# Rewriting a two-block attention kernel: B's keys and values first, and one unit-by-unit schedule for sliding-window attention with the other products between

## The chip, the cores and the metric

One core of one Trainium2 chip runs the kernel. The metric is the device time of one execution in microseconds. The kernel before has a median of 465.69 us over 6 runs (463.81 to 466.82).

## The reference

Two independent blocks read their own x (2048 tokens, 640 channels, bf16) and write the two halves of an output of 2048 x 1280. Both project x to q, k and v with 32 heads of 20 channels.

Block A is attention in a window of 256 tokens; block B is linear attention:

```python
# A
scores = einsum("bhqd,bhkd->bhqk", q, k) * (Dh ** -0.5)
mask = (q_idx - k_idx >= 0) & (q_idx - k_idx < 256)
p = softmax(where(mask, scores, -1e9)); o = p @ v;  a = o @ wo
# B
phi = lambda t: where(t > 0, t + 1, exp(t)) + 1e-6
kv = einsum("bhsd,bhse->bhde", phi(k), v);  z = phi(k).sum(over tokens)
o = (phi(q) @ kv) / (phi(q) @ z + 1e-6);  b = o @ wo
```

## The kernel before, in words

The tile framework places instructions by a scheduler; the program text sets priority, and stages follow each other nearly as written.

1. `load_inputs` (L92) transposes x of A by DMA on the SP queue (L98) and loads wqkv and wo. It is called again for B before the attention.
2. `proj_channel_major` (L109) makes q and k of A with channels on partitions: 5 chunks of 4 x 5 matmuls of 512 columns (L129), an eviction of 2048 columns (L139, L141), and then small DMAs on three queues (L163) that move each head's 20 channels to a 32-partition slot of `q_pad` or `k_pad`. Four heads share a tile of 128 partitions.
3. `proj_token_major` (L165) makes v of A with tokens on partitions (L180, L190) and puts a column of ones behind each head's 20 channels, so that the product with v also gives the denominator.
4. The attention of A (L278 to L335) goes by 16 blocks of 128 queries and in each by steps of 3 heads: up to 9 score products of 128 columns with 20 rows (L288), one exponential of up to 1152 columns on ACT (L297), a mask product on DVE for the oldest key block (L301) and one for the diagonal block (L307), and 9 value products with the probabilities as weights and 21 columns (L317). Division by the denominator is at L325 and L328.
5. `tail` (L208) transposes A's output on TensorE (L220), evicts it (L224), multiplies with wo (L229), evicts (L237) and stores. B's queries (L129 again, with exp and relu at L144 and L146) run in the same stretch.
6. B's keys and values (L369), their phi (L378 to L390), the kv sum per group of four heads (L403, L412), the products with phi(q) (L426), the division (L435 to L439) and B's `tail`.

All of a stage's buffers are opened and closed with the stage. Scores have 2 PSUM buffers.

Of the kernel before, what the change touches and what calls it, by code (L numbers as in the profile page):

```python
# [8 lines left out]
P = 128  # L9
ALU = mybir.AluOpType  # L10
ACT = mybir.ActivationFunctionType
BF16 = mybir.dt.bfloat16
F32 = mybir.dt.float32


@with_exitstack
def kernel(
# [10 lines left out]
    nc = tc.nc  # L28
    _, S, D = A_x.shape
    H = 32  # L30
    Dh = D // H
    HD = 32
    HV = Dh + 1
    HG = H // 4
    KT = D // P
    NT = S // P
    NQ = 512
    NQT = S // NQ
    assert S % NQ == 0 and D % P == 0 and H * Dh == D and Dh < HD
    scale = float(Dh) ** -0.5  # L40
    out2 = out[0]
    xA = A_x[0]
    xB = B_x[0]

    def head_pieces(c):
        pieces = []
        for h in range(H):
            r0 = h * Dh
            r1 = r0 + Dh
            lo = max(r0, c * P)  # L50
            hi = min(r1, (c + 1) * P)
            if lo < hi:
                pieces.append((h, lo - c * P, hi - lo, lo - r0))
        return pieces

    head_steps = []
    h0 = 0
    while h0 < H:
        nh = min(3, H - h0)
        head_steps.append((h0, nh))  # L60
        h0 += nh

    const = ctx.enter_context(tc.tile_pool(name="const", bufs=1, side="left"))
    ident = const.tile([P, P], BF16, name="ident")
    make_identity(nc, ident[:])
    maskD = const.tile([P, P], BF16, name="maskD")
    nc.gpsimd.memset(maskD[:], 1.0)
    nc.gpsimd.affine_select(
        out=maskD[:],
        in_=maskD[:],  # L70
        pattern=[[1, P]],
        compare_op=ALU.is_ge,
        fill=0.0,
        base=0,
        channel_multiplier=-1,
    )
    maskE = const.tile([P, P], BF16, name="maskE")
    nc.gpsimd.memset(maskE[:], 1.0)
    nc.gpsimd.affine_select(
        out=maskE[:],  # L80
        in_=maskE[:],
        pattern=[[-1, P]],
        compare_op=ALU.is_ge,
        fill=0.0,
        base=-1,
        channel_multiplier=1,
    )
    woA_sb = const.tile([P, KT, D], BF16, name="woA_sb")
    woB_sb = const.tile([P, KT, D], BF16, name="woB_sb")
    otokA = const.tile([P, NT, D], BF16, name="otokA")  # L90

    def load_inputs(stack: ExitStack, name, x_ap, wqkv_ap, wo_ap, wo_tile):  # L92
        inp = stack.enter_context(tc.tile_pool(name=name, bufs=1, side="right"))
        xT = inp.tile([P, KT, S], BF16, name=f"xT_{name}")
        w = inp.tile([P, KT, 3 * D], BF16, name=f"w_{name}")
        xv = x_ap.rearrange("s (c p) -> s c p", p=P)
        for c in range(KT):
            nc.sync.dma_start_transpose(out=xT[:, c, :], in_=xv[:, c, :])  # L98
        wv = wqkv_ap.rearrange("(kt p) n -> p kt n", p=P)
        for i in range(3):  # L100
            nc.sync.dma_start(
                out=w[:, :, i * D : (i + 1) * D], in_=wv[:, :, i * D : (i + 1) * D]
            )
        nc.sync.dma_start(out=wo_tile[:], in_=wo_ap.rearrange("(kt p) n -> p kt n", p=P))
        return xT, w

    dma_engines = [nc.sync, nc.scalar, nc.gpsimd]

    def proj_channel_major(  # L109
        name, xT, w, col_base, pads, mode, psum_bufs, stage_bufs, sbuf_side="right"  # L110
    ):
        with ExitStack() as stack:
            psq = stack.enter_context(
                tc.tile_pool(name=f"psq_{name}", bufs=psum_bufs, space=bass.MemoryType.PSUM, side="left")
            )
            stage = stack.enter_context(
                tc.tile_pool(name=f"stage_{name}", bufs=stage_bufs, side=sbuf_side)
            )
            scr = None
            if mode == "phi":  # L120
                scr = stack.enter_context(
                    tc.tile_pool(name=f"scr_{name}", bufs=1, side=sbuf_side)
                )
            dcount = 0
            for c in range(KT):
                ps = psq.tile([P, NQT, NQ], F32, name="ps")
                for nt in range(NQT):
                    for kt in range(KT):
                        nc.tensor.matmul(  # L129
                            ps[:, nt, :],  # L130
                            lhsT=w[:, kt, col_base + c * P : col_base + (c + 1) * P],
                            rhs=xT[:, kt, nt * NQ : (nt + 1) * NQ],
                            start=(kt == 0),
                            stop=(kt == KT - 1),
                        )
                chunk = stage.tile([P, S], BF16, name="chunk")
                cv = chunk[:].rearrange("p (n f) -> p n f", f=NQ)
                if mode == "scale":
                    nc.scalar.activation(out=cv, in_=ps[:], func=ACT.Copy, scale=scale)  # L139
                elif mode == "copy":  # L140
                    nc.any.tensor_copy(out=cv, in_=ps[:])  # L141
                elif mode == "phi":
                    e = scr.tile([P, NQT, NQ], BF16, name="e")
                    nc.scalar.activation(out=e[:], in_=ps[:], func=ACT.Exp)  # L144
                    r = scr.tile([P, NQT, NQ], BF16, name="r")
                    nc.scalar.activation(out=r[:], in_=ps[:], func=ACT.Relu)  # L146
                    nc.vector.tensor_scalar(
                        out=cv,
                        in0=e[:],
                        scalar1=1e-6,  # L150
                        scalar2=1.0 + 1e-6,
                        op0=ALU.add,
                        op1=ALU.min,
                    )
                    nc.vector.tensor_tensor(out=cv, in0=cv, in1=r[:], op=ALU.add)
                else:
                    raise ValueError(mode)
                for h, src_row, cnt, dst_off in head_pieces(c):
                    hg, j = divmod(h, 4)
                    dst = pads[hg][HD * j + dst_off : HD * j + dst_off + cnt, :]  # L160
                    eng = dma_engines[dcount % len(dma_engines)]
                    dcount += 1
                    eng.dma_start(out=dst, in_=chunk[src_row : src_row + cnt, :])  # L163

    def proj_token_major(name, xT, w, col_base, dstv_fn, mode, psum_bufs):  # L165
        with ExitStack() as stack:
            pst = stack.enter_context(
                tc.tile_pool(name=f"pst_{name}", bufs=psum_bufs, space=bass.MemoryType.PSUM, side="left")
            )
            scr = None  # L170
            if mode == "phi":
# [94 lines left out]
    with ExitStack() as at:  # L266
# [8 lines left out]
        def oslot(h):  # L275
            return (h % 2) * 16 + h // 2
# [199 lines left out]
```

## Time and profile before

| | |
|---|---|
| median of 6 runs | 465.69 us (463.81 to 466.82) |
| profiled execution | 466.82 us, span 465.0 us |
| mean granted TensorE clock | 0.769 of full speed |
| TensorE (PE) busy | 391.0 us, 84% |
| weight loads (PEld) | 224.5 us, 48% |
| VectorE (DVE) | 195.2 us, 42% |
| ScalarE (ACT) | 274.7 us, 59% |
| GpSimd (POOL) | 25.8 us, 6% |
| DMA | 25.56 MB in 34,361 packets |

PE busy time covers overlapping matmuls with modelled ends, so it says that the engine was occupied and not that it ran at its peak. Busy shares are means over stages that differ a good deal, and have to be read stage by stage.

### The profile page before, as it was taken

How to read it: one execution, taken by the hardware profiler on the slowest of the kernel's cores; microseconds unless marked ns; L12 is line 12 of the kernel's file. 1: busy time of each engine (PE TensorE's matmuls, PEld its weight loads, DVE VectorE, ACT ScalarE, POOL GpSimd, SP SyncE). 2: the span in 40 equal slices, each digit the busy share in tenths (PEclk: the TensorE clock that was granted, in tenths of full speed). 3: DMA queues.
4: the chain of work that ended last, by engine and by line, in shares of the span. 5: the costliest groups of instructions: out<-in, count | busy, mean ns of one | idle time of the engine just before them, and what ended most of it. 6: DMA issues, size and time to landing. Idle time of an engine off the chain costs nothing. (4 is left out here: it accounts for less than half of the span.)

```text
span 465.0 us, 10106 instructions
## 1 busy us (share of the span) xinstructions
PE 391.0 (84%) x4316; PEld 224.5 (48%) x4316; DVE 195.2 (42%) x497; ACT 274.7 (59%) x322; POOL 25.8 (6%) x48
## 2 busy tenths in 40 slices
PE   0298989989999999999999999889866999839975
PEld 0143435545555556555555555444422555626542
DVE  0000151056665655566566666714411322228721
ACT  1034103589888898998888886651434767442222
POOL 1012221000000000000000002200101000000000
PEclk9999999965555555555555555999978999968999
DMA  8954351097000000000000000033221000001111
GB/s 162 301 167 130 81 138 54 1 207 234 1 3 1 4 2 1 3 1 1 4 2 1 3 1 1 30 92 114 88 79 53 4 0 1 1 1 43 58 62 67
DMA packets 34361, 25.56 MB, mean 55 GB/s; under 512 B 23180, under 2 KB 32396, under 8 KB 34316
## 3 DMA queue, kind: packets, MB, share of 16 engines
q1 hardware_dynamic: 31628, 19.65, 15.4%
q0 software_dynamic: 1632, 2.61, 2.3%
q10 hardware_dynamic: 1056, 2.66, 2.2%
q8 instruction: 34, 0.56, 0.5%
q14 instruction: 11, 0.09, 0.1%
HBM read 6.55 MB, written 5.24 MB: 25 GB/s over the span
## 5 line engine op out<-in xcount | busy, mean ns | idle before, releaser
L297 ACT ACTIVATE p<-S_ps 128x1152 bf16<-128x1152 f32 (+3 forms) x176 | 173.5, 1042 | 20.3 <-PE S_ps L288 16.2
L288 PE MATMUL S_ps<-q_pad,k_pad 20*128 20x128 bf16 x1440 | 116.9, 289 | 15.6 <-ACT p L297 13.7
L317 PE MATMUL O_qb<-vaugA,p 128*128 128x21 bf16 x1440 | 96.2, 185 | 1.6 <-DVE p L307 0.8
L317 PEld LDWEIGHTS <-p 128*128 128x128 bf16 x1440 | 64.4, 106 | 56.0 <-DVE p L301 27.0
L301 DVE TENSOR_TENSOR p<-p,maskE 128x384 bf16<-128x384 bf16 (+1 forms) x154 | 54.0, 351 | 57.6 <-ACT p L297 56.6
L307 DVE TENSOR_TENSOR p<-p,maskD 128x384 bf16<-128x384 bf16 (+1 forms) x176 | 60.8, 346 | 24.7 <-ACT p L297 24.2
L129 PE MATMUL ps<-xT_inA,w_inA 128*128 128x512 bf16 x200 | 46.0, 394 | 21.8 <-DMA w_inA<-in_A_wqkv_dram 19.8
L288 PEld LDWEIGHTS <-k_pad 20*128 20x128 bf16 x1440 | 46.1, 104 | 29.4 <-issue 18.9
L369 PE MATMUL pstkv<-w_inB,xT_inB 128*128 128x512 bf16 (+1 forms) x240 | 45.1, 352 | 3.8 <-ACT r L146 3.8
L237 ACT CAST osb<-pso 128x640 bf16<-128x640 f32 x25 | 17.4, 694 | 51.3 <-PE pso L229 39.1
L129 PEld LDWEIGHTS <-w_inA 128*128 128x128 bf16 x200 | 20.1, 101 | 47.2 <-DMA w_inA<-in_A_wqkv_dram 19.8
L229 PEld LDWEIGHTS <-oT_cmp 128*128 128x128 bf16 x320 | 24.1, 98 | 34.9 <-DVE oT_cmp L224 12.0
L369 PEld LDWEIGHTS <-xT_inB 128*128 128x128 bf16 x240 | 24.0, 100 | 25.1 <-issue 5.2
L141 DVE CAST chunk<-ps 128x2048 bf16<-128x2048 f32 x4 | 9.2, 2292 | 57.7 <-PE ps L129 57.7
L129 PE MATMUL ps<-xT_inB,w_inB 128*128 128x512 bf16 x100 | 28.9, 435 | 3.7 <-ACT r L146 3.7
L229 PE MATMUL pso<-woB_sb,oT_cmp 128*128 128x512 bf16 (+1 forms) x160 | 26.0, 305 | 6.1 <-DVE oT_cmp L224 4.8
L139 ACT ACTIVATE chunk<-ps 128x2048 bf16<-128x2048 f32 x5 | 9.4, 1877 | 34.5 <-PE ps L129 29.4
L229 PE MATMUL pso<-woA_sb,oT_cmp 128*128 128x512 bf16 (+1 forms) x160 | 24.5, 300 | 5.3 <-ACT oT_cmp L224 2.9
L190 ACT CAST vaugA<-pst 128x640 bf16<-128x640 f32 x14 | 9.7, 696 | 28.9 <-PE pst L180 28.9
L180 PE MATMUL pst<-w_inA,xT_inA 128*128 128x512 bf16 (+1 forms) x160 | 21.9, 299 | 2.4 <-DVE chunk L141 2.4
L378 ACT ACTIVATE et<-pstkv 128x640 bf16<-128x640 f32 x16 | 11.3, 704 | 14.8 <-PE pstkv L369 14.8
L224 DVE COPY oT_cmp<-T 128x640 bf16<-128x640 bf16 x22 | 10.8, 489 | 20.5 <-PE T L220 20.3
(47 smaller groups left out, 240.6 us busy)
## 6 DMA issues: line engine op xcount, KB each, us to landing
out_dram<-osb SPq DMA_DIRECT2D x32, 160.0 KB
w_inA<-in_A_wqkv_dram SPq DMA_DIRECT2D x3, 800.0 KB
w_inB<-in_B_wqkv_dram SPq DMA_DIRECT2D x3, 800.0 KB
woA_sb<-in_A_wo_dram SPq DMA_DIRECT2D x1, 800.0 KB
woB_sb<-in_B_wo_dram SPq DMA_DIRECT2D x1, 800.0 KB
q_pad<-chunk SPq DMA_DIRECT2D x10, 80.0 KB
q_pad<-chunk POOLq DMA_DIRECT2D x10, 80.0 KB, 3.8
k_pad<-chunk SPq DMA_DIRECT2D x10, 80.0 KB
```

The source lines that it names most:

```text
L129: nc.tensor.matmul(ps[:, nt, :], lhsT=w[:, kt, col_base + c * P : col_base + (c + 1) * P], rhs=xT[:, kt, nt * NQ : (nt + 1) * NQ], start=( ...
L180: nc.tensor.matmul(ps[:, n0:n1], lhsT=xT[:, kt, tb * P : (tb + 1) * P], rhs=w[:, kt, col_base + n0 : col_base + n1], start=(kt == 0), stop ...
L224: nc.any.tensor_copy(out=oT[:], in_=T2[:])
L229: nc.tensor.matmul(pso[:, n0:n1], lhsT=oT[:, c, :], rhs=wo_sb[:, c, n0:n1], start=(c == 0), stop=(c == KT - 1),)
L237: nc.any.tensor_copy(out=osb[:], in_=pso[:, 0:D])
L288: nc.tensor.matmul(S_ps[:, i, kbi, :], lhsT=k_pad[hg][HD * j : HD * j + Dh, kb * P : (kb + 1) * P], rhs=q_pad[hg][HD * j : HD * j + Dh, qb ...
L297: nc.scalar.activation(out=p[:, 0:nh, 0:nkb, :], in_=S_ps[:, 0:nh, 0:nkb, :], func=ACT.Exp)
L301: nc.vector.tensor_tensor(out=p[:, 0:nh, 0, :], in0=p[:, 0:nh, 0, :], in1=maskE[:, None, :].to_broadcast([P, nh, P]), op=ALU.mult,)
L307: nc.vector.tensor_tensor(out=p[:, 0:nh, nkb - 1, :], in0=p[:, 0:nh, nkb - 1, :], in1=maskD[:, None, :].to_broadcast([P, nh, P]), op=ALU.mult,
L317: nc.tensor.matmul(O_qb[:, oslot(h), 0:HV], lhsT=p[:, i, kbi, :], rhs=vaugA[:, kb, h * HV : (h + 1) * HV], start=(kbi == 0), stop=(kbi == ...
L369: nc.tensor.matmul(ps[:, n0:n1], lhsT=xTB[:, kt, tb * P : (tb + 1) * P], rhs=wB[:, kt, D + n0 : D + n1], start=(kt == 0), stop=(kt == KT - 1),
L378: nc.scalar.activation(out=e[:], in_=kv_view, func=ACT.Exp)
```

## The change

The whole function is rewritten for the same result, with the program order of each engine kept as written (`manual_schedule`). Its parts:

- B's keys and values come first, token block by token block, with phi(k) as max(min(exp, 1) + eps, x + 1 + eps); the kv sum accumulates in PSUM in groups of 6 heads with a mask afterwards. The masked kv is multiplied with wo of B into one 640 x 640 matrix `mB`, and the key sums become `zmat`, so that B's output is (phi(q) divided by its denominators) @ `mB`.
- A's q and k of a quarter (512 tokens) go to DRAM in one DMA and come back in four that place heads in 32-partition slots.
- A's attention goes by 4 quarters x 8 groups of 4 heads x 6 units. A unit has two heads' scores of up to 512 columns each in two PSUM banks, one exponential of up to 1024 columns, diagonal masks on DVE, old-edge masks by affine_select on POOL. Value products have v as weights (21 columns of 32) and up to 384 columns of probabilities, four heads on four column groups, channels on partitions.
- Denominators go through DRAM to a dense layout, are inverted and split in three bf16 parts, come back, and are spread over channels by a product with a selection matrix.
- A's next quarter, B's queries, B's denominators and both output projections are a queue of filling that is emitted between units by a budget of columns. x of B is transposed by DMA a second time for the queries.

The diff cut to its core (everything of the old body goes; B's lead, one of each helper and the loop are shown):

```diff
+    sp.dma_start(out=xn[:], in_=xB[0:NQ, :].rearrange("(i p) n -> p i n", p=P))
+    act.dma_start(out=wkB[:], in_=wview(B_wqkv, D, 2 * D))
+    act.dma_start(out=wvB[:], in_=wview(B_wqkv, 2 * D, 3 * D))
...
+    for t in range(1, 4):
+        load_xT(t, xB, t)
+    sp.dma_start(out=wA[:], in_=wview(A_wqkv, 0, 3 * D))
...
+    for tb in range(16):
...
+        for h in range(2):
...
+        for h, (c0, c1) in enumerate(((0, 360), (360, 640))):
...
+        if tb > 0:
+            kvT(tb - 1)
+        if tb == 3:
+            load_xT(0, xA, 0)
...
+    def a_qk(gp, t, w, c, slot, eng):
...
+        if c == KT - 1:
+            d = qkd[t % 2][w]
+            sp.dma_start(out=d[:].rearrange("(c p) n -> p c n", p=P), in_=stg[w][:])
+            dst = qt[t % 2] if w == 0 else kt_[t % 3]
+            dv = d[:].rearrange("(g j e) n -> j e g n", j=4, e=DH)
+            for j in range(4):
+                sp.dma_start(out=dst[32 * j : 32 * j + DH, :, :], in_=dv[j])
...
+    sps = ctx.enter_context(
+        tc.tile_pool(name="sps", bufs=2, space=PSUM, side="left", reuse_waits="tile")
...
+    gp = ctx.enter_context(
+        tc.tile_pool(name="gp", bufs=4, space=PSUM, side="right", reuse_waits="tile")
...
+    def emit_S(n):
+        t, hg, u, items = units[n]
+        ps = sps.tile([P, 2, NQ], F32, name="S")
...
+                pe.matmul(
+                    ps[:, i, col : col + nq],
+                    lhsT=kt_[(kb // 4) % 3][
+                        32 * j : 32 * j + DH, hg, (kb % 4) * P : (kb % 4 + 1) * P
+                    ],
+                    rhs=qt[t % 2][32 * j : 32 * j + DH, hg, q0 : q0 + nq],
                     start=True,
                     stop=True,
+                    tile_position=(32 * j, 0),
                 )
...
+        if t > 0:
+            act.activation(out=p[:], in_=ps[:], func=ACT.Exp, scale=scale)
...
+    def selE(ap, n):
+        pool.affine_select(
+            out=ap, in_=ap, pattern=[[0, n], [-1, P]], compare_op=ALU.is_ge,
+            fill=0.0, base=-1, channel_multiplier=1,
+        )
+
+    def mulD(ap, n):
+        dve.tensor_tensor(
+            out=ap, in0=ap, in1=maskD[:].unsqueeze(1).to_broadcast([P, n, P]), op=ALU.mult
+        )
+
+    def emit_mask(n):
...
+    def g_pv(t, hg):
...
+            for j in range(4):
+                h = 4 * hg + j
+                p, i = where[(t, h, ty)]
+                pe.matmul(
+                    ps[32 * j : 32 * j + 32, q0 : q0 + nq],
+                    lhsT=vaug[(kb // 4) % 3][:, kb % 4, h * 21 : h * 21 + 32],
+                    rhs=p[:, i, col : col + nq],
+                    start=(k == 0),
+                    stop=(k == len(todo) - 1),
+                    tile_position=(0, 32 * j),
+                    skip_group_check=True,
+                )
...
+        half = 2 * t + hg // 4
+        dve.tensor_copy(out=oF[half % 3][:, hg % 4, :], in_=ps[:])
+        if hg % 4 == 3:
+            normA(half)
...
+        later(2, den_in)
+        later(4, rec)
+        later(6, rec_in)
+        for g in range(4):
+            later(14 + g // 2, lambda g=g: mul(g))
+        later(16, compact)
+        if i == 1:
+            later(18, obf_in)
...
+    fill = [
+        load(0, xA, 2) + A_tile(1, 1) + load(1, xB, 2) + QB_tile(0, 2) + load(2, xA, 3)
+        + QB_tile(1, 3) + load(3, xB, 3) + DEN(0),
+        A_tile(2, 0) + OB(0) + DEN(1) + OA(0),
+        A_tile(3, 2) + QB_tile(2, 1) + OA(1) + DEN(2),
+        OB(1) + QB_tile(3, 3) + DEN(3) + OB(2),
+    ]
...
+    for n in range(n_units):
+        step[0] = n
...
+            left_cols = sum(c for _, c in fill[t]) + 8 * 1536
+        emit_mask(n)
+        if n + 2 < n_units:
+            if (n + 2) % per == 0:
+                flush()
+            emit_S(n + 2)
+            emit_exp(n + 2)
+        run_pending()
+        if u == 5:
+            pv_wait.append((n + 2, t, hg))
+        if pv_wait and pv_wait[0][0] <= n:
+            _, tt, hh = pv_wait.popleft()
+            if cur[0] is not None:
+                queue.appendleft((cur[0], 0))
+                cur[0] = None
+            run(g_pv(tt, hh))
+            left_cols -= 1536
+        budget = max(0, left_cols) / (per - n % per)
+        fill_pe(budget)
...
+    flush()
+    queue.extend(OA(2) + OB(3))
+    while pending:
+        step[0] += 1
+        run_pending()
+        fill_pe(5 * HALF)
+    queue.extend(OA(3))
+    flush()
```

`later(k, f)` emits f some 1.5 k units on. `A_tile(t, slot)` is the q, k and v of quarter t of A (25,600 + 12,800 columns), `QB_tile` phi(q) of B (12,800), `DEN` B's denominators, `OA` and `OB` the output projections (12,800 each).

## Rows read from the trace of the kernel before

**Rows 1.** Busy time by stage: window, its length, busy us (count) by engine, clock, DMA

```profile
core 0: us, PE busy (x) PEld busy (x) DVE busy (x) ACT busy (x) POOL busy (x), PEclk, DMA share, GB/s
0.00:19.80 19.80, 0.00 (x0) 0.00 (x0) 0.48 (x1) 1.28 (x1) 1.52 (x10) 1.00 0.89 208
19.80:94.50 74.70, 68.42 (x369) 32.86 (x369) 11.51 (x8) 22.30 (x23) 12.11 (x24) 1.00 0.39 108
94.50:293.00 198.50, 183.21 (x2891) 112.24 (x2892) 121.17 (x364) 172.18 (x173) 4.94 (x1) 0.51 0.11 27
120.00:160.00 40.00, 36.98 (x600) 22.84 (x597) 23.82 (x74) 35.62 (x35) 0.00 (x0) 0.50 0.01 2
293.00:354.70 61.70, 48.90 (x324) 24.73 (x322) 21.61 (x31) 29.22 (x27) 4.76 (x10) 0.94 0.26 78
354.70:401.90 47.20, 45.09 (x240) 24.00 (x240) 14.43 (x33) 31.89 (x48) 2.46 (x4) 0.96 0.04 12
440.00:465.00 25.00, 16.02 (x130) 9.12 (x130) 3.93 (x8) 6.51 (x10) 0.00 (x0) 1.00 0.19 66
```

**Rows 2.** Timeline, first 20 us: SP's transposes and PE's first products

```profile
0.81 11.97 SPq L98 DMA_TRANSPOSE xT_inA<-in_A_x_dram  x5
19.81 20.38 PE L129 MATMUL ps<-xT_inA,w_inA 128*128 128x512 bf16 x82 [19.81 <-DMA w_inA<-in_A_wqkv_dram]
```

**Rows 3.** Chain of waits, in order of time: start, length, what

```profile
354.68 45.12 PE pstkv L369 x240
```

**Rows 4.** ACT groups by form: busy us, mean ns, idle before and its releaser

```profile
L297 ACT ACTIVATE p<-S_ps 128x1152 bf16<-128x1152 f32 x140 | 151.0, 1129 | 18.3 <-PE S_ps L288 14.5 <-ACT p L297 3.8
L297 ACT ACTIVATE p<-S_ps 128x768 bf16<-128x768 f32 x24 | 18.7, 806 | 0.9 <-PE S_ps L288 0.7
L297 ACT ACTIVATE p<-S_ps 128x512 bf16<-128x512 f32 x1 | 0.6, 591 | 0.0
```

**Rows 5.** DMA issues: KB each, median us from issue to landing

```profile
q_pad<-chunk POOLq DMA_DIRECT2D x10, 80.0 KB, 3.8
q_pad<-chunk POOLq DMA_DIRECT2D x1, 32.0 KB, 2.5
```

**Rows 6.** DVE groups by form

```profile
L307 DVE TENSOR_TENSOR p<-p,maskD 128x256 bf16<-128x256 bf16 x16 | 4.6, 285 | 0.1
L237 DVE CAST osb<-pso 128x640 bf16<-128x640 f32 x7 | 5.8, 825 | 17.4 <-PE pso L229 17.4
L141 DVE CAST chunk<-ps 128x2048 bf16<-128x2048 f32 x4 | 9.2, 2292 | 57.7 <-PE ps L129 57.7
L382 DVE TENSOR_SCALAR pk_pad<-et 128x640 bf16<-128x640 bf16 x16 | 5.4, 335 | 28.4 <-ACT et L378 28.4
L147 DVE TENSOR_SCALAR chunk<-e 128x2048 bf16<-128x2048 bf16 x5 | 3.6, 729 | 14.0 <-ACT e L144 14.0
L325 DVE RECIPROCAL recipA<-O_qb 128x32 f32<-128x32 f32 x16 | 5.7, 358 | 13.8 <-PE O_qb L317 13.8
```

**Rows 7.** Timeline of PE in the attention: start, length of the merged run, count

```profile
203.47 0.40 PE L288 MATMUL S_ps<-q_pad,k_pad 20*128 20x128 bf16 x6
203.82 0.23 PE L317 MATMUL O_qb<-vaugA,p 128*128 128x21 bf16 x2
203.98 0.29 PE L288 MATMUL S_ps<-q_pad,k_pad 20*128 20x128 bf16 x3
204.21 0.36 PE L317 MATMUL O_qb<-vaugA,p 128*128 128x21 bf16 x7
204.52 0.40 PE L288 MATMUL S_ps<-q_pad,k_pad 20*128 20x128 bf16 x6
```

**Rows 8.** POOL group by form

```profile
L79 POOL TENSOR_SCALAR_AFFINE_SELECT maskE<-maskE 128x128 bf16<-128x128 bf16 x1 | 0.3, 292 | 0.1
```

**Rows 9.** Chain of waits at the end of the span

```profile
459.58 1.55 PE pso L229 x10
461.20 0.69 ACT osb L237
```

More of the change, by code (lines that the diff above doesn't have):

```diff
@@ L1 @@
+from collections import deque
 from contextlib import ExitStack
@@ L13 @@
 F32 = mybir.dt.float32
+DRAM = bass.MemoryType.DRAM
+PSUM = bass.MemoryType.PSUM
+H = 32
+DH = 20
+D = 640
+S = 2048
+KT = 5
+NQ = 512
+NTT = 4
+HG = 8
+HALF = 320
+EPS = 1e-6
 @with_exitstack
@@ L416 @@
[L416 to L429 removed]
+    pe, act, dve, pool, sp = nc.tensor, nc.scalar, nc.vector, nc.gpsimd, nc.sync
@@ new lines @@
+    for c in range(KT):
+        run(a_qk(gp2, 0, 1, c, 0, "act" if c % 2 else "dve"))
+    sp.dma_start(out=zd[:], in_=zs[120:121, :])
+    sp.dma_start(out=zcol[:], in_=zd[0].rearrange("(c p) -> p c", p=P))
+    for g in range(6):
+        n = 120 if g < 5 else 40
+        for h in range(2):
+            ps = gp2.tile([P, NQ], F32, name="g")
+            pe.matmul(
+                ps[0:n, 0:HALF],
+                lhsT=kvbd[0:n, g * 120 : g * 120 + n],
+                rhs=woB[0:n, g, h * HALF : (h + 1) * HALF],
+                start=True,
+                stop=True,
+            )
+            act.copy(msb[0:n, g, h * HALF : (h + 1) * HALF], ps[0:n, 0:HALF])
@@ new lines, with runs @@
+    units = []
+    for t in range(NTT):
+        for hg in range(HG):
+            items = [(4 * hg + j, ty) for ty in range(3) for j in range(4)]
+            for u in range(6):
+                units.append((t, hg, u, items[2 * u : 2 * u + 2]))
+    where = {}
+    s_tiles = {}
+    def runs(items):
+        r = []
+        for i, (_, ty) in enumerate(items):
+            if r and r[-1][0] == ty:
+                r[-1][2] = i + 1
+            else:
+                r.append([ty, i, i + 1])
+        return r
@@ new lines, in g_out @@
+    def g_out(lhs, w, tb, h, col0):
+        i = tb % 4
+        ps = gp.tile([P, NQ], F32, name="g")
+        for c in range(KT):
+            pe.matmul(
+                ps[:, 0:HALF],
+                lhsT=lhs[:, c, i * P : (i + 1) * P],
+                rhs=w[:, c, h * HALF : (h + 1) * HALF],
+                start=(c == 0),
+                stop=(c == KT - 1),
+            )
+            if c < KT - 1:
+                yield HALF
+        if h == 0:
+            ocount[0] += 1
+        o = osb[ocount[0] % 3]
+        if h == 0:
+            act.copy(o[:, h * HALF : (h + 1) * HALF], ps[:, 0:HALF])
+        else:
+            dve.tensor_copy(out=o[:, h * HALF : (h + 1) * HALF], in_=ps[:, 0:HALF])
+        if h == 1:
+            sp.dma_start(out=out2[tb * P : (tb + 1) * P, col0 : col0 + D], in_=o[:])
+        return HALF
@@ new lines, with fill_pe, flush @@
+    queue = deque()
+    cur = [None]
+    debt = [0]
+    def fill_pe(budget):
+        debt[0] += budget
+        while queue and debt[0] > 0:
+            gen, cost = queue.popleft()
+            run(gen)
+            debt[0] -= cost
+        if not queue:
+            debt[0] = 0
+    def flush():
+        while queue or cur[0] is not None:
+            fill_pe(1 << 30)
+    n_units = len(units)
+    per = n_units // NTT
+    pv_wait = deque()
+    emit_S(0)
+    emit_S(1)
+    emit_exp(0)
```

804 lines of the change are left out of this document (426 added, 378 removed).

## The prediction

> **What bounds the kernel now.** I read the busy time by stage first [rows 1]: the reader is to see that no engine bounds the whole. Up to 19.8 us nothing computes: TensorE waits for the transposed x and the first weights [rows 2]. From there to 94.5 A's projections keep PE busy 68.4 of 74.7 us while ACT has 22.3 and DVE 11.5. In the attention of A, 94.5 to 293, ACT is the densest that works without pause (172.2 of 198.5 us, 87%; its exponentials are most of it); PE shows 183.2 us busy but at a granted clock of 0.51, its lower level of 1.2 GHz. After 293 come 172 us of B and of both output projections, where PE does the work again and ACT and DVE follow it; the chain of waits there is PE work with short evictions between [rows 3, 9], and one stretch of it gives PE's real rate: 240 matmuls of L369, 102,400 columns, in 45.12 us, 2.27 columns per ns [rows 3]. So the kernel is dense matmul stages and an exp stage laid end to end. Profiled time 466.8 us, span 465.0, so 1.8 us lie around the span; the median of the runs shown is 465.7, within 0.3% of it.
>
> **The change part by part.** Three parts: B's keys and values with A's first quarter (lead), A's attention in 4 quarters of 48 units with everything else as filling (middle), and the end of the last quarter (tail).
>
> *Lead.* Before the first product xn, wkB and wvB must land: 2.3 MB, at 208 GB/s (the first stage's mean [rows 1]) 11 us, less if the load goes faster after the transposes; five transposes of 2048 rows took 11.97 us of SP issue [rows 2], so 15 of 512 rows take some 9 us on SP, behind xn and beside the ACT queue's weights. Start at 12 us. Then 16 blocks of 6,400 columns, as many as L369 has, 45.1 us, with 640 more each for kvT (10,240, 4.5 us): 62 us. ACT's four evictions per block (two of 320, 360, 240 columns at 0.16 us and 0.84 ns a column, from the 1152 and 768 forms [rows 4]) are 1.7 us and DVE's 1.7 us, under PE's 3.1, so they hide. A's q and k of the first quarter, 25,600 columns, 11.3 us: 73. Then k goes to DRAM and back in two hops; landings of 32 and 80 KB took 2.5 and 3.8 us [rows 5], and 0.65 MB a hop is more, so 4.5 us each: 82. The 12 products of M and the v of the quarter (16,640 columns, 7.3 us) fit into that wait, which without them would be idle PE. First exponential near 84 us, with B's keys, values and kv sum done before it.
>
> *Middle, ACT.* The scores are the same 184,320 columns. 144 units have one exponential of 1024 columns, 1.02 us by the forms; the 48 of the first quarter are 16 of 768 (0.81), 16 of 1024 and 16 of 512 (0.59) [rows 4]. That is 38.7 us for the first quarter and 49.1 for each other. Added: 20 exponentials of 512 for B's queries (10, 0, 5, 5 by quarter) and 20 output copies of 320 (0.43 us; 0, 8, 4, 8). Sum 44.6, 52.6, 53.8, 55.6.
>
> *Middle, DVE.* Durations from [rows 6]: mask products of 256 columns 0.285; evictions from PSUM 0.158 us and 1.04 ns a column by the 640 and 2048 casts, so 0.69 for 512 and 0.49 for 320; the bf16 tensor_scalar 0.30 for 512. A quarter has 64 mask products (18.2 us), 8 evictions of the value products (5.5), up to 8 normalising products (5.5), A's next quarter in the first three (10 of 512 and 8 of 320: 10.8), B's queries (1.0 each), B's normalising (0.69 each), output copies and three small reciprocal chains (1.2 each, from the 0.36 us reciprocal and five small operations). Sum 49.6, 54.5, 50.6, 48.7.
>
> *Middle, PE.* Filling 64,640 columns in each of the first three quarters and 39,040 in the last, 2,000 to 9,200 for the spreading of reciprocals, scores 36,864 then 3 x 49,152, value products as many. In the trace nine score products of 128 columns on three row groups and nine value products alternate [rows 7]: six score products from 203.47 to 203.82 us take 0.35, where 768 columns one after the other at 1.2 GHz are 0.64; small tiles overlap by 1.83. The four column groups of the new value products are not shown: between 1 (none overlap) and 4; I take 1.83, the nearest row. At 2.27 columns per ns: 47.1, 56.2, 53.9, 44.9 us; with the bounds 1 and 4 for the value products, sums of 239 and 178 instead of 202.
>
> *Middle, POOL.* 64 affine_selects of 256 columns a quarter (32 in the first). The trace has 128 columns at 0.29 us [rows 8]; 256 lie between 0.29 and 0.58, so 19 to 37 us a quarter, below the other engines. The cover is that value products come two units later.
>
> So ACT, DVE and PE have 207, 203 and 202 us, all within a few per cent, in order, with two score buffers. The quarter costs the longest of the three: 49.6, 56.2, 53.9, 55.6, together 215 us. They won't mesh fully: in the attention stage ACT, with the most work, is busy 0.87 of it, and 35.6 of 40 us in its even part, 0.89 [rows 1]. I take 215/0.89 = 242 us. The bounds: 207 (ACT alone, no pause), 269 where the value products don't overlap at all (quarters of 54.5, 66, 63.7 and 55.6, over 0.89; a total of 388), and what PE needs at the other clock (below).
>
> Hidden at nothing: q and k for the next quarter through DRAM (ready some 20 units before use), the transposes and the detours on SP (some 15 MB in 242 us, 62 GB/s, beside the 208 GB/s shown), the reciprocals' way through DRAM, given 21 units. Each detour adds a wait on SP: four reads wait for the write, some 4 us, and behind them in SP's queue stand the next transposes, the denominators and the output stores. Those are due 20 units later or hold one of three osb buffers; if that cover is gone, rival 3 has the price.
>
> *Tail.* After the last value product: eviction 0.7, six DRAM hops of 3 us (2.5 to 3.8 for small ones), reciprocals 1.2, four normalising products 3, output projection of 8 half blocks 5.6, copy 0.5 and, as now, 3 us from the last copy to the end of the span [rows 9]: 32, and 1 for the last mask and product. The two other output projections (25,600 columns, 11 us) lie inside the hops. If the clock falls in the hops, 5 us more.
>
> Sum: 84 + 242 + 33 + 2 around the span = 361, say 362 us.
>
> **The clock.** The attention stage shows 0.51 though PE was never idle for long (183 of 198.5 us busy), and the dense stages show 1.00 or near [rows 1]. The Trainium skill ("TensorE: Matmul & The Clock Gate", Part 1) says that the clock falls after the engine has been idle and rises with sustained work; the trace disagrees here, since the stage was busy and slow. By the page the new middle runs at full speed and the sum is 362.
> By the row, products of 20 rows or 21 columns alone leave the clock low, and no row shows a mixture; at the low level the sum is rival 4's 506. In the new units about half of PE's time is full 128-row products of the kind that ran at 1.00, so I take the full clock, least surely in the last quarter, which has the least filling.
>
> **The rivals.**
> 1. ACT alone bounds the middle: 84 + 207 + 33 + 2 = 326 us. For it: PE and DVE have less work than ACT in sum. Against: 0.87 to 0.89 in the trace with less coupling.
> 2. Masks on DVE and POOL take turns: both are released by the same exponential. If each mask product waits out one select of 0.44 us (the middle of its bounds), DVE gains 28 us a quarter (14 in the first): 63.6, 82.5, 78.6, 76.7, sum 301, total 420. The skill ("SBUF — State Buffer", Who interferes with whom) states such an exclusive lock between a VectorE instruction with two SBUF inputs and a GpSimd one that reads SBUF; no row here has the two together. Against it: products that find POOL idle wait nothing.
> 3. The one SP queue holds q, k, denominators and outputs behind each other, and a quarter starts late: 10 us each, about 402. For it: every hop waits on SP for the one before; against: the distances above.
> 4. Slower: PE's clock stays at 1.2 GHz through the middle. Its 459,000 effective columns then take 382 us, total 84 + 382 + 38 + 2 = 506. For it: 0.51 in the stage that has these small products now; against: half of the work is dense. It decides from a middle of 343 us (466.8 - 2 - 84 - 38).
> 5. The change doesn't do what it says: the filling (233,000 columns, 103 us) doesn't run beside an attention of today's 198 us. 84 + 198 + 103 + 33 + 2 = 420. Program order has filling in most units, so I give it no chance of its own; it shares rival 2's number.
>
> **How the numbers follow.** Forecast 0.50 (its own range 340 to 390), rival 1 0.15, rival 2 0.12, rival 3 0.11, rival 4 0.12. The range goes from 322 (rival 1, a little better) to 450 (rivals 2 and 3, with value products that don't overlap); rival 4 and a small rest of rival 1 are left out, under 0.2. Within 0.5% (2.3 us, about what a measurement can tell from no change) lies only a partly slow clock: 0.02. Slower 0.12, faster 0.86.
>
> **What would show it.** First exponential near 84 us; a middle of some 240 us with ACT busy over 0.85; granted clock near 1.0 there; mask products at 0.285 us and not waiting for POOL; the last 33 us mostly DMA waits on the chain. I am wrong if the clock in the middle is near 0.5, if a quarter takes over 70 us, or if DVE waits for selects.

## The result and the profile after

The changed kernel takes 366.3 us (median of 8 runs, 365.22 to 368.02) where the kernel before takes 465.2 (16 runs): a ratio of 0.787 [0.786, 0.789]. The profiled execution took 367.41 us, its span 365.7. The forecast was 362, inside 340 to 390.

The stages of the kernel after, in the columns of [rows 1]. The lines are the lead (up to the first exponential of the attention), the four quarters and the tail:

```profile
0.00:81.70 81.70, 71.50 (x540) 48.95 (x540) 39.51 (x105) 36.38 (x85) 11.85 (x32) 1.00 0.72 176
81.70:139.50 57.80, 51.57 (x403) 18.95 (x404) 40.08 (x112) 41.26 (x58) 13.88 (x32) 0.88 0.60 118
139.50:202.80 63.30, 58.13 (x582) 24.65 (x581) 53.08 (x144) 49.18 (x57) 25.96 (x64) 0.95 0.38 100
202.80:264.40 61.60, 57.27 (x572) 23.56 (x570) 48.35 (x130) 49.98 (x58) 26.67 (x64) 0.94 0.31 81
264.40:327.60 63.20, 51.04 (x526) 20.79 (x525) 49.51 (x135) 50.12 (x62) 26.97 (x64) 0.89 0.20 57
327.60:365.70 38.10, 21.72 (x148) 13.39 (x148) 12.60 (x28) 5.23 (x13) 0.41 (x1) 0.82 0.30 91
```

The gain is read from three differences. Before, 94.5 us lie ahead of the attention, 198.5 in it and 172 behind it [rows 1]; now it is 81.7, 245.9 and 38.1. So 134 us behind and 13 ahead were saved, and the attention became 47 us longer: 99 us in all, the difference of the spans. The work from behind the attention now runs in it, on a TensorE whose granted clock went there from 0.51 to 0.88 and more.

The middle is 245.9 us, forecast 242. But the table doesn't show the forecast's reason: ACT is busy 0.71 to 0.81 of the quarters (forecast over 0.85), and PE 0.81 to 0.93. The groups by form of the kernel after (columns of [rows 4]) answer for the operations that the trace of before did not have, or had elsewhere [rows 6, 8]:

```profile
L431 ACT ACTIVATE pb<-S 128x1024 bf16<-128x1024 f32 x144 | 140.8, 1042 | 28.6 <-PE S L413 11.9 <-POOL pb L440 10.2 <-issue 5.4
L440 POOL TENSOR_SCALAR_AFFINE_SELECT pb<-pb 128x256 bf16<-128x256 bf16 x224 | 93.9, 429 | 221.1 <-ACT pb L435 111.7 <-ACT pb L431 107.6
L446 DVE TENSOR_TENSOR pb<-pb,maskD 128x256 bf16<-128x256 bf16 x256 | 71.9, 319 | 2.3 <-ACT pb L431 2.2
L492 DVE RECIPROCAL denA<-denA 128x64 f32<-128x64 f32 x8 | 4.4, 547 | 10.5 <-DMA denA<-dend 10.5
```

The reader is to see the idle times: ACT has 28.6 us, from three causes, and DVE waits 10.5 us at a reciprocal for the denominators that come from DRAM, 7.1 of them in the middle, in three waits. Such a wait is small against 245.9, but here is what one looks like. First DVE, then SP's queue, then PE, all of the kernel after, near 310 us (start, length of the merged run, what, and the idle time ahead of it):

```profile
307.71 0.47 DVE L446 TENSOR_TENSOR pb<-pb,maskD 128x256 bf16<-128x256 bf16 x2
311.95 0.55 DVE L492 RECIPROCAL denA<-denA 128x64 f32<-128x64 f32 x1 [3.77 <-DMA denA<-dend]
313.81 0.68 DVE L487 COPY oF<-g 128x512 f32<-128x512 f32 x1
314.41 0.89 DVE L446 TENSOR_TENSOR pb<-pb,maskD 128x256 bf16<-128x256 bf16 x4
```

```profile
303.70 0.58 SPq L500 DMA_DIRECT2D dend<-oF  x1
306.61 0.34 SPq L610 DMA_DIRECT2D recdB<-rsB  x1
307.65 0.47 SPq L505 DMA_DIRECT2D denA<-dend  x1
308.28 1.27 SPq L615 DMA_DIRECT2D rec3B<-recdB  x3
```

```profile
312.61 1.01 PE L619 MATMUL g<-rec3B,selB 96*128 96x512 bf16 x2 [1.97 <-DVE denA L492]
314.54 1.49 PE L548 MATMUL g<-mB,pq 128*128 128x320 bf16 x5 [0.92 <-DVE oF L487]
```

And the same stretch by windows of 4 us (columns of [rows 1]):

```profile
306.00:310.00 4.00, 2.54 (x41) 1.32 (x40) 2.15 (x9) 3.01 (x5) 1.22 (x3) 1.00 0.45 112
310.00:314.00 4.00, 1.40 (x6) 0.39 (x6) 1.87 (x7) 2.03 (x3) 1.94 (x5) 0.70 0.48 151
314.00:318.00 4.00, 3.46 (x30) 1.17 (x32) 4.00 (x13) 1.76 (x3) 0.25 (x1) 0.50 0.19 59
318.00:322.00 4.00, 3.48 (x43) 1.55 (x35) 3.88 (x11) 2.65 (x4) 1.10 (x4) 0.95 0.19 53
```

The reciprocal is emitted six units after the eviction that gives the denominators. Their write to DRAM was issued at 303.70, but the DMA that brings them back stood on SP behind the one of B's reciprocals (306.61), was issued at 307.65 and landed at 311.9. DVE ran nothing for 3.77 us; an eviction and four masks written behind the reciprocal ran from 313.81 on, and PE had 1.40 us of work in a window of 4. Then PE's granted clock went to 0.50, the lower level, and the next five products of 320 columns took 1.49 us, where five take 0.85 in the stretch quoted further down. There are six such stretches in the middle (from 82, 126, 142, 250, 266 and 310 us), each behind windows that PE did not fill: at 82 k came back from DRAM, at 250 PE waited for ACT, and in the other four DVE ran a chain of reciprocals or waited for denominators. The instructions that stood still behind three of these chains, at 126, 142 and 266 us, name DVE as their releaser:

```profile
126.90 0.60 ACT L583 ACTIVATE eq<-g 128x512 bf16<-128x512 f32 x1 [3.29 <-DVE pq L587]
144.11 2.29 PE L253 MATMUL g<-xT,wA 128*128 128x512 bf16 x5 [2.15 <-DVE obp L519]
267.95 1.49 PE L548 MATMUL g<-mB,pq 128*128 128x320 bf16 x5 [1.54 <-DVE obp L519]
```

Worked out from the mean clocks of the table, TensorE is at the lower level in 2 x (57.8 x 0.12 + 63.3 x 0.05 + 61.6 x 0.06 + 63.2 x 0.11) = some 41 us of the middle, which costs up to 21.

### The profile page after: what moved, and what is told of

Same layout as the page of the kernel before. It is cut to its first block, busy times and chain, and to the rows that moved or that the text cites. A ratio compares the mean times of both kernels' runs of the same rounds, so it can differ in the third digit from the quotient of the medians.

```text
span 365.7 us, 7554 instructions
## 1 busy us (share of the span) xinstructions
PE 311.2 (85%) x2768; PEld 150.3 (41%) x2768; DVE 243.1 (66%) x648; ACT 232.1 (63%) x329; POOL 105.7 (29%) x256
## 4 chain that ended last, share of the span: by engine, by line
PE 62%; DVE 13%; DMA 11%; ACT 8%; issue 4%; SPq 1%; POOL 1%; ACTq 0%; DVEq 0%
PE g L253 12%; PE g L548 11%; PE S L413 10%; PE g L202 6%; PE g L226 6%; ACT pb L431 6%; PE g L476 6%; PE g L278 4%; PE g L573 3%; DMA denA<-dend 2%; DVE pb L446 2%; DVE obp L519 2%; DMA qkd<-stg 2%; DMA kt<-qkd 2%; DMA xn<-in_B_x_dram 2%
## 5 line engine op out<-in xcount | busy, mean ns | idle before, releaser
L431 ACT ACTIVATE pb<-S 128x1024 bf16<-128x1024 f32 x144 | 140.8, 1042 | 28.6 <-PE S L413 11.9
L440 POOL TENSOR_SCALAR_AFFINE_SELECT pb<-pb 128x256 bf16<-128x256 bf16 x224 | 93.9, 429 | 221.1 <-ACT pb L435 111.7
L413 PE MATMUL S<-qt,kt 20*128 20x256 bf16 (+2 forms) x704 | 67.2, 285 | 20.5 <-ACT pb L431 10.4
L446 DVE TENSOR_TENSOR pb<-pb,maskD 128x256 bf16<-128x256 bf16 x256 | 71.9, 319 | 2.3 <-ACT pb L431 2.2
L253 PE MATMUL g<-xT,wA 128*128 128x512 bf16 x200 | 51.7, 399 | 3.0 <-DVE obp L519 2.1
L435 ACT ACTIVATE pb<-S 128x768 bf16<-128x768 f32 (+2 forms) x48 | 36.9, 818 | 14.5 <-PE S L413 13.9
L548 PE MATMUL g<-woA,obf 128*128 128x320 bf16 x160 | 29.1, 335 | 10.8 <-DMA obf<-od 10.0
L548 PE MATMUL g<-mB,pq 128*128 128x320 bf16 x160 | 28.8, 318 | 5.0 <-DVE oF L487 1.9
L476 PE MATMUL g<-pb,vaug 128*32 128x256 bf16 (+2 forms) x704 | 28.9, 297 | 1.6 <-DVE pb L446 0.8
L573 PE MATMUL g<-xT,wqB 128*128 128x512 bf16 x100 | 26.7, 400 | 0.0
L548 PEld LDWEIGHTS <-obf 128*128 128x128 bf16 x160 | 15.8, 107 | 22.0 <-DMA obf<-od 10.5
```

The source lines that it names most:

```text
L253: pe.matmul(ps[:], lhsT=wA[:, kt, w * D + c * P : w * D + (c + 1) * P], rhs=xT[slot][:, kt, :], start=(kt == 0), stop=(kt == KT - 1),)
L413: pe.matmul(ps[:, i, col : col + nq], lhsT=kt_[(kb // 4) % 3][32 * j : 32 * j + DH, hg, (kb % 4) * P : (kb % 4 + 1) * P], rhs=qt[t % 2][32 ...
L431: act.activation(out=p[:], in_=ps[:], func=ACT.Exp, scale=scale)
L435: act.activation(out=p[:, a:b, 0:w], in_=ps[:, a:b, 0:w], func=ACT.Exp, scale=scale)
L440: pool.affine_select(out=ap, in_=ap, pattern=[[0, n], [-1, P]], compare_op=ALU.is_ge, fill=0.0, base=-1, channel_multiplier=1,)
L446: dve.tensor_tensor(out=ap, in0=ap, in1=maskD[:].unsqueeze(1).to_broadcast([P, n, P]), op=ALU.mult)
```

## Experiments

Two theories. **A** is the forecast's: ACT, DVE and PE have nearly the same work, and the quarter costs the longest of them over 0.89; less work on the longest engine shortens it until the next one bounds. **B**: PE bounds, with pauses and a low clock in a few stretches; their cause is the order of DVE and SP around the reciprocals. Stages are given as lead | four quarters | tail; the kernel after is 81.7 | 57.8, 63.3, 61.6, 63.2 | 38.1. Where no interval is given there was one run, unless its range is given. Repeated runs of one kernel lie 1 to 6 us apart here, in experiment 9 13 us, so a few microseconds in a quarter of a single run are not clear of noise. Neither theory forecast the sizes well; each experiment says where they missed.

**1. Half the exponentials** (of each head's 512 columns in the last three quarters, 256 are left out; buffers are cleared first).

```diff
-            act.activation(out=p[:], in_=ps[:], func=ACT.Exp, scale=scale)
+            act.activation(out=p[:, :, 0:256], in_=ps[:, :, 0:256], func=ACT.Exp, scale=scale)
```

> Leaves out half of the exponentials' columns in quarters 2 to 4 (256 of 512 a head; the other half of the probabilities is stale). ACT's work falls from 52.6, 53.8 and 55.6 us a quarter to about 32, 33 and 35. Theory A (three engines close together, the longest of them at 0.89): PE and DVE, unchanged, set the pace; the middle goes from 246 to about 238 us, all of it in the last quarter. Theory B (PE with its pauses and its slow clock sets the middle, in a few episodes): under 4 us are gained, or something is lost if PE waits for nothing new. Rival 1 (ACT alone bounds): some 15 us less in each of three quarters, 320 us in all.

Measured: 367.5 us; 93.0 (the clears) | 55.4, 62.8, 58.0, 59.3 | 37.3. Its second quarter:

```profile
148.40:211.20 62.80, 56.44 (x578) 24.28 (x581) 52.71 (x141) 30.08 (x56) 27.35 (x71) 0.92 0.39 102
```

ACT's work fell from 49.2 to 30.1 us and the quarter by 0.5; the other two fell by 3.6 and 3.9, and the first, where ACT has all its work, by 2.4. The middle is 235.5 us, 10.4 less, where A had expected 8, all in the last quarter, and B under 4: neither is met. But 18 to 19 us less of ACT's work a quarter gave at most 4, so ACT alone doesn't bound the middle.

**2 and 3. No selects, or no masks** (the old-edge masks on POOL are left out, then instead the diagonal masks on DVE).

```diff
     def selE(ap, n):
+        return
...
     def mulD(ap, n):
+        return
```

> Leaves out the window's old-edge masks on POOL (224 affine_selects). Theory A: mask products on DVE go from 0.319 to 0.285 us, 9 us of DVE in all, and the time falls by 2 to 5 us. Theory B: ACT's 10 us of waits for POOL go too, but the pauses of PE stay, so under 5 us. Rival 2 (masks of DVE and POOL take turns): 20 us or more.

> Leaves out the diagonal mask products on DVE (256 of 0.319 us, 82 us of DVE by the trace, 20 a quarter). Theory A: ACT and PE set the pace as before, so 0 to 5 us less. Theory B: DVE gets out of its bursts sooner and PE's pauses shorten: 8 to 15 us less. If DVE were the bound: 40 us or more.

Measured: 360.1 us, 81.2 | 57.7, 62.1, 58.9, 60.5 | 38.0 without selects; 359.8 us, quarters of 57.2, 62.0, 59.2, 60.5, without masks. Masks in the first of the two:

```profile
L447 DVE TENSOR_TENSOR pb<-pb,maskD 128x256 bf16<-128x256 bf16 x256 | 62.6, 282 | 2.9 <-ACT pb L431 2.7
```

With POOL silent a mask takes 282 ns on average instead of 319, as before the change (285 in [rows 6]). The single masks (shortest, median and longest in ns), in the kernel after and then without selects, show that most are as quick as before and some wait:

```profile
L446 DVE TENSOR_TENSOR pb<-pb,maskD x256: 273/283/531, 86.5 to 328.5; 128x256 bf16<-128x256 bf16 x128
L447 DVE TENSOR_TENSOR pb<-pb,maskD x256: 277/282/293, 85.9 to 321.0; 128x256 bf16<-128x256 bf16 x128
```

So the two engines do hinder each other, by 37 ns a mask on average, 9 us of DVE and at most 6 us of the time. Taking some 15 us of DVE out of each full quarter gave no more, 6.5 us, where A had expected 0 to 5 and B 8 to 15. DVE's load doesn't bound either.

**4. Short filling** (in B's queries and in all output projections one of five partial products is left).

```diff
-        for c in range(KT):
+        for c in range(1):
```

> Leaves out 4 of the 5 partial products of B's queries and of both output projections; schedule, evictions and DMAs stay. PE has 9 us less in each of the first three quarters and 13.5 less in the last, and some 13 less in the tail's projections. Theory A: PE no longer is the longest anywhere, ACT and DVE are (54 to 56 a quarter), so the middle falls by 3 to 6 us. Theory B or PE as the bound: the middle falls by 20 us or more, unless the thinner filling lets the clock fall to 1.2 GHz, which would show as a granted clock below 0.9 in the last quarter.

Measured: 364.3 us; 80.8 | 55.4, 66.8, 62.6, 63.3 | 33.7; clock in the quarters 0.75, 0.76, 0.77, 0.50. The last quarter:

```profile
265.60:328.90 63.30, 54.27 (x442) 16.09 (x441) 48.80 (x135) 51.22 (x62) 27.10 (x64) 0.50 0.20 56
```

The reader is to see 84 products fewer than after, and the same 63 us. PE is busy 54 us of them at the lower level. The clock is far below 0.9, which B had named as its exception; so this run doesn't decide between A and B. The filling that was taken out had paid for itself by the clock.

**5. All work but PE's thinned** (half the exponentials, no masks, no selects, by the edits of 1 to 3).

> Leaves out half of the exponentials' columns in quarters 2 to 4, all mask products and all selects together (12 clears of buffers come ahead of the attention and lengthen the lead by 11 us). ACT and DVE are down to some 33 us a quarter. Theory A: PE alone is left and takes its sum, 47, 56, 54 and 45 us by quarter, 202, give or take 5%. Theory B: PE's pauses at the reciprocals and the slow clock behind them stay, so the middle is 215 to 230. If units wait on something else, the middle stays at 235 or more.

Measured: 358.5 us; 94.0 | 55.0, 59.9, 55.2, 55.2 | 37.1. Its second and last quarter, and its wait for denominators (us in all, times, longest):

```profile
149.00:208.90 59.90, 56.24 (x578) 24.32 (x581) 36.36 (x74) 30.05 (x57) 0.00 (x0) 0.94 0.40 107
264.10:319.30 55.20, 47.03 (x540) 19.92 (x545) 33.70 (x71) 31.98 (x61) 0.00 (x0) 0.91 0.23 65
```

```profile
DVE denA L496 <- DMA denA<-dend: 18.6, 6, 5.0
```

The middle is 225.3 us, although ACT and DVE now have at most 41 us in any quarter. The expectation had A at PE's own sum of 202, and B at 215 to 230. This speaks only against an A without any pauses: with the forecast's own factor A gives 202/0.89 = 227, by quarter 52.9, 63.1, 60.6 and 50.4, which meets the sum and misses the quarters by 2 to 5 us. What the run shows is that of 245.9 us PE's products in their order, with PE's pauses and its clock, take 225. It also shows that DVE's wait by itself is no measure: it is 18.6 us here, more than the 10.5 of the kernel after, in a middle that is 20.6 shorter, with no masks behind the reciprocal.

**6. B behind the attention** (B's queries, denominators and outputs after the last unit).

```diff
-        A_tile(2, 0) + OB(0) + DEN(1) + OA(0),
+        A_tile(2, 0) + load(0, xB, 2) + OA(0),
...
-        OB(1) + QB_tile(3, 3) + DEN(3) + OB(2),
+        [],
```

> B's queries, denominators and outputs (89,600 columns of filling) go behind A's attention; A's next quarters and A's outputs stay in it. Theory A and B: the middle falls by 10 to 25 us (PE has 11, 6, 6 and 17 us less by quarter), with a granted clock near 0.5 in the last quarter, which has no filling; some 40 us of products and 10 to 20 us of waits come behind: 385 to 410 us. If filling costs its full time wherever it stands: about 366.

Measured: 395.4 us; 81.0 | 55.5, 57.4, 62.0, 53.5 | 84.3. The last quarter, which has no filling left:

```profile
255.90:309.40 53.50, 39.09 (x392) 12.64 (x390) 31.22 (x96) 45.34 (x49) 28.46 (x64) 0.51 0.13 35
```

B between the units is worth 28 us of the span: 46 in the tail, less 17.5 in the quarters and 0.7 in the lead. A quarter with nothing between its units takes 53.5 us, at 0.51, with ACT busy 0.85 of it. Both theories had expected this (385 to 410 us); 366, filling at its full price wherever it stands, is refuted. An estimate from the quarter: three of these and a first with three quarters of the columns are some 200 us, as much as the attention before (198.5). So the new units are not quicker by themselves; what is gained in the middle is what runs between them.

**7. Filling ahead of the first scores** (four parts of A's second quarter before the first unit, while k is on its way through DRAM).

```diff
+    pre = A_tile(1, 1)
+    for gen, _ in pre[:4]:
+        run(gen)
```

> Four chunks of the filling (5 products of 512 columns each, 4.8 us) go ahead of the first scores, into the wait for k's way through DRAM. Theory B: PE keeps its clock there (0.53 to 0.61 from 82 to 90 us now), so 3 to 5 us less. Theory A without the clock: the chunks fill 3 us of idle PE, but PE is not alone on the path: 0 to 2 us less.

Measured: 363.4 us, ratio 0.778 [0.774, 0.782]; 82.6 | 54.7, 63.0, 59.4, 65.0 | 37.5. That is the low end of B's 3 to 5 us, but not by B's reason. PE now works in the pause before the first quarter (it was nearly idle from 78 to 84 us); its clock fell all the same, to 0.50 from 86 to 90 us, because DVE met another way through DRAM first, that of B's key sums, and PE waited 3.0 us for an eviction that stood behind it:

```profile
86.92 0.51 DVE L339 TENSOR_TENSOR zmat<-sel,zcol 128x160 bf16<-128x160 bf16 x1 [9.79 <-DMA zcol<-zd]
88.09 2.29 PE L253 MATMUL g<-xT,wA 128*128 128x512 bf16 x5 [3.00 <-DVE stg L265]
```

The first quarter gained 3.1 us. How much of it is the work moved into the pause (4 us of PE) was not separated.

**8. Reciprocals spread** (one DVE operation a unit, and A's starting 11 units after the eviction instead of 6, B's likewise; the products that use them stay 21 units after).

```diff
-        later(4, rec)
-        later(6, rec_in)
+            for k in range(6):
+                pending.append((step[0] + 11 + k, lambda k=k: rec_op(k)))
+            pending.append((step[0] + 18, rec_in))
```

> Puts the reciprocals' chains of DVE one operation per unit instead of six at once, and A's first one 11 units after the denominators leave instead of 6. Theory A: no operation goes, so 0 to 2 us less. Theory B: DVE no longer stands in its queue for the denominators (10.5 us in four waits, three of them in the middle) nor runs chains of 3.4 us ahead of the masks; the episodes with PE pauses and a granted clock of 0.5 to 0.6 near 126, 142, 250, 266 and 312 us go, 2 to 3 us each: 8 to 14 us less.

Measured: 379.5 us, ratio 0.813 [0.808, 0.819]; 81.6 | 51.8, 74.1, 71.7, 58.6 | 40.7. The waits of this kernel (engine, line, waited for: us in all, times, longest):

```profile
PE g L527 <- DMA rec<-recd: 26.1, 7, 7.6
```

Both theories had expected less time, A 0 to 2 us, B 8 to 14; it is 13 us more. The first and the last quarter, which have none of A's output projections between their units, gained 6.0 and 4.6 us: the stall on DVE is real. In the others the reciprocals now came back from DRAM after PE wanted them, and of the 26 us that PE stood for them 19.6 lie there. The wait had moved.

**9. Spread, and used later** (edit of 8 with the chain from 9 units, and A's products 25 units after, B's 17).

> The reciprocal chains spread over units as before, but the products that spread them over the channels wait longer: A's 25 units after the denominators leave (21 before the edit), B's 17 (9). In the first spreading PE stood 26 us for reciprocals on their way, in quarters 2 and 3, while quarters 1 and 4 took 51.8 and 58.6 us instead of 57.8 and 63.2. Theory B: without that wait quarters 2 and 3 gain as the other two did, about 4 us each; the middle is 226 to 232 and the time 348 to 354. Theory A: the gain of quarters 1 and 4 was chance, 362 or more.

Measured: 364.0 us, with runs from 355.16 to 368.54, too far apart for an interval; 82.5 | 52.3, 73.5, 61.6, 55.1 | 37.8. The time is in A's range (362 or more), not in B's (348 to 354), but A's reason, chance, doesn't hold: the first and the last quarter keep their gain. The third is where the change had it, where B had 4 us less. In the second, of a run of 364.5 us, PE waited 2.5 us for reciprocals and 3.2 us for A's output, which the filling there wanted as early as before, and the clock was 0.50 from 178 to 182 and from 190 to 202 us. Whether the run of 355.16 lacked these waits isn't known.

**10. Spread, prefilled, output in parts** (9 and 7 together, A's output read back in two parts, half of B's last output projection kept for the tail).

> The later products, the four chunks of filling ahead of the first scores, A's output read back from DRAM in two parts (2 and 3 of 5 chunks), and half of B's last output projection placed behind the last reciprocals' products, in the wait for A's output. Theory B: 3 us less in the first quarter, and in the tail 1 us of DMA and 2 to 3 us of slow clock in the last projection (8.0 us now, 5.6 at 2.4 GHz) on top of the run with the later products: 342 to 348. If these waits only change places: the same as that run.

Measured: 358.7 us, ratio 0.768 [0.763, 0.773]; 82.3 | 52.1, 68.7, 63.5, 56.4 | 35.1. That is 11 us above the top of what B expected and 5 below the run before, by the second and third quarter: PE still waits 8.3 us for reciprocals.

**11 and 12. A's output projections a quarter later**, with all of 10 and products 30 units after (11), and alone on the kernel after (12).

```diff
-        A_tile(2, 0) + OB(0) + DEN(1) + OA(0),
-        A_tile(3, 2) + QB_tile(2, 1) + OA(1) + DEN(2),
-        OB(1) + QB_tile(3, 3) + DEN(3) + OB(2),
+        A_tile(2, 0) + OB(0) + DEN(1),
+        OA(0) + A_tile(3, 2) + QB_tile(2, 1) + DEN(2),
+        OA(1) + OB(1) + QB_tile(3, 3) + DEN(3) + OB(2),
```

> The combined version with A's output projections one quarter later (OA(0) first in the third quarter, OA(1) first in the fourth; filling 64,640, 51,840, 64,640 and 51,840 columns instead of 64,640, 64,640, 64,640 and 39,040), and with the spreading products 30 units after the denominators. Theory B: the second quarter, 63 to 74 us in the runs so far and the one where PE waited for reciprocals or for A's output, has no such wait left and falls to 55 to 58; the others stay at 52, 61 and 58: 340 to 348 us. If these waits move once more: 355 to 360, as in the combined version.

> The changed kernel with A's output projections one quarter later as its only edit. Theory A (the longest engine's sum by quarter): quarters 2 and 4 change places, 6 us less and 6 us more, and the time stays within 2 us of 366. Theory B: episodes stay where DVE holds the others, so also 362 to 368; a fall below 360 would say that the projections themselves waited for A's output.

Measured for 11: 351.4 us, ratio 0.757 [0.754, 0.760], the best version, 15 us below the change; 82.8 | 52.3, 56.1, 61.8, 59.3 | 36.5. Its second to fourth quarter, and its reciprocal:

```profile
135.10:191.20 56.10, 51.70 (x539) 21.11 (x539) 46.96 (x130) 46.86 (x54) 26.45 (x63) 0.97 0.40 102
191.20:253.00 61.80, 57.31 (x576) 23.74 (x576) 50.47 (x137) 50.21 (x59) 26.57 (x65) 0.97 0.33 88
253.00:312.30 59.30, 53.60 (x571) 23.48 (x573) 46.46 (x134) 51.91 (x65) 26.59 (x63) 0.94 0.23 65
```

```profile
L493 DVE RECIPROCAL denA<-denA 128x64 f32<-128x64 f32 x8 | 4.3, 543 | 1.5 <-DMA denA<-dend 1.5
```

The wait for denominators fell from 10.5 to 1.5 us, the time at the lower level, worked out as above, from 41 to 21, and the middle from 245.9 to 229.5. Every operation of the change is still in the kernel, but four chunks of filling (4 us of PE) stand in the lead now. B had the quarters about right (55 to 58 for the second; 52, 61 and 58) and the total too low (340 to 348). Measured for 12: 379.7 us, ratio 0.816 [0.814, 0.818]; 82.0 | 57.3, 61.1, 72.2, 67.3 | 38.3. Its waits, and the longest of them on SP, DVE and PE:

```profile
DVE denA L492 <- DMA denA<-dend: 18.0, 5, 8.7
```

```profile
245.66 0.59 SPq L500 DMA_DIRECT2D dend<-oF  x1
250.25 0.38 SPq L531 DMA_DIRECT2D obf<-od  x1
250.73 0.46 SPq L505 DMA_DIRECT2D denA<-dend  x1
254.76 0.55 DVE L492 RECIPROCAL denA<-denA 128x64 f32<-128x64 f32 x1 [8.70 <-DMA denA<-dend]
257.18 2.29 PE L573 MATMUL g<-xT,wqB 128*128 128x512 bf16 x5 [7.09 <-DVE oF L487]
```

The same move alone costs 13 us, which neither theory expected (A 364 to 368, B 362 to 368). The read of the denominators stood on SP behind that of A's output, 5 us after their write was issued; DVE, which still wants them after six units, stood for 8.7 us, and PE for 7.1 us for an eviction behind that reciprocal. So B's mechanism is seen at work in both runs, though its numbers were not met: time is lost where the first instruction that needs what comes from DRAM is too near to the write. Run 11 makes five edits at once, and what each is worth in it was not separated.

## Why the prediction was right, point by point

**Lead, 84 forecast, 81.7 measured.** Errors cancel here in part. The first product with B's weights ran at 8.6 us, not 12. The two hops of k took 6.8 and 5.9 us, as the chain of waits after shows, against 4.5 each in the sum, which went by landings of an eighth of the size and less [rows 5]:

```profile
70.19 6.80 DMA qkd<-stg
78.14 5.88 DMA kt<-qkd
```

The second ends at 84.0, but the first exponential needs only two of its four parts and ran at 81.7. The fifteen transposes, put at some 9 us of SP, ran for 22.2 us, which PE's first blocks hid.

**Middle, 242 forecast, 245.9 measured.** The quarters were forecast at 55.7, 63.1, 60.6, 62.5 and measured at 57.8, 63.3, 61.6, 63.2. ACT's exponential was right (1.02 forecast, 1042 ns), the select too (0.44; 429 ns), the mask product not (0.285; 319 ns, as experiment 2 answers), and the sums by engine within some 6 us but for the first quarter's DVE (49.6 forecast, 40.1 busy). The step that was wrong in its reason is the factor 0.89, taken from ACT's share in an attention that ACT led. Here PE is busy 51.6, 58.1, 57.3 and 51.0 us, 218 of 245.9, which is 0.89 as well: the number came out, with another engine and another cause, and that is luck. Of those 218 up to 21 are the lower clock, which leaves some 197 at full clock beside the 202 of the forecast; the rest is PE's pauses. Read as ACT's, the factor would send one to ACT for the next gain, where experiment 1 found at most 4 us a quarter.

**Overlap of small products.** I took 1.83 for both kinds, from a stretch at the lower clock. A stretch of the kernel after at full clock (PE's timeline: start, length, what):

```profile
184.87 0.39 PE L413 MATMUL S<-qt,kt 20*128 20x128 bf16 x4
185.19 0.84 PE L476 MATMUL g<-pb,vaug 128*32 128x384 bf16 x24
185.97 0.85 PE L548 MATMUL g<-mB,pq 128*128 128x320 bf16 x5
```

The 24 value products, 6,144 columns, run from 185.19 to 185.97: 2.56 us one after the other at 2.4 GHz, so an overlap of 3.3 on the four column groups. The four score products, 1,024 columns, take 0.32 us where 0.43 would be one after the other: 1.33. The two misses cancel nearly.

**The reciprocals' way, hidden at nothing.** This step failed. I gave it 21 units, from the eviction to the products. DVE's own reciprocal comes after six, and whatever stands behind it in DVE's order waits too. Experiments 8, 11 and 12 show its price: up to 6 us a quarter where the wait and the chains in one go are taken away, and with the rest of the order set to match, 16 us in the middle, some 3 of them by the chunks that experiment 7 moves.

**The clock.** The full clock was taken for the middle and 0.88 to 0.95 came, falling in the six stretches told above. Where the filling is thin or missing it is at the lower level, as in the attention before: 0.50 and 0.51 in the last quarters of experiments 4 and 6, with PE busy 54 of 63 and 39 of 53 us, beside 0.89 with 51 of 63 in the kernel after. So rival 4 had a real mechanism, and the dense filling is what kept it away. In experiment 6 PE also has 14 us of pauses, so that row doesn't tell the kind of product from the idle time. Experiment 4's row disagrees, as the stage of before did, with what the Trainium skill says ("TensorE: Matmul & The Clock Gate", Part 1), that the clock falls after idleness and rises with sustained work, while the stretch at 310 us agrees with it.

**Other rivals.** Rival 1 (ACT alone bounds): no, by experiment 1. Rival 2 (masks and selects take turns): some masks wait (the longest 531 ns, the median 283), on average 37 ns, at most 6 of the 58 us that it needed. Rival 3 (SP's queue): it is there, but a quarter doesn't start late by it; in the change it is part of DVE's 10.5 us, and in experiment 12, for 13 us in all, the read of the denominators stands behind that of A's output. Rival 5: the filling does run beside the attention, worth 28 us for B's part alone.

**Tail, 33 forecast, 38.1 measured.** Its end, from the chain of waits of the kernel after:

```profile
347.43 2.40 DMA od<-obp
350.03 4.38 DMA obf<-od
354.46 8.02 PE g L548 x40
```

The last projection was forecast at 5.6 us and took 8.0, since PE had waited 10 us for its input and started at the lower clock; this was named as "if the clock falls in the hops, 5 us more" and left out of the sum. The hop ahead of it took 4.4 instead of 3.

**Open.** Of the 99 us that the change gains, experiment 6 tests the 28 of B's part alone; the rest is read from the stages. How the 21 us between 245.9 and 225.3 divide between ACT's and DVE's work and the clock was not separated. Why the runs of experiment 9 lie 13 us apart wasn't found.

## What to carry to other kernels

Where engines run in written order, count the distance of a way through DRAM to the first instruction that touches what comes back, on whichever engine, and not to the last one that uses it. A wait of 4 us on one engine can cost PE nearly as much again afterwards (from 310 us on, 7 us at the lower level, up to 3.4 lost), so look for windows of low clock and ask what PE did just before. And when a wait is moved, look at the whole order again: two of the reorderings here were slower than what they were to mend (379.5 and 379.7 us against 366.3), and the one in which the distances fitted together gained 15 us.

## What the runs showed of the hardware

The price of four products side by side on 32 columns each: 6,144 columns in 0.78 us. Taking work from PE can gain nothing: experiment 4 left out four fifths of the products of B's queries and of the output projections, the clock fell from 0.89 to 0.50 in the last quarter, and the quarter stayed at 63 us. And masks on DVE are slowed by POOL's selects, from 282 to 319 ns on average, a few to as much as 531 while the median stays; the selects are slowed by the masks, from 408 ns to 429.
